# Attention ahead of two expert layers: chunks of both batches in turn, a packed state, and a new first order

## The chip, the cores and the metric

One core of one Trainium2 chip runs the whole program. The time is the device time of one execution in microseconds (us), and the number compared is the median of several executions.

## What is computed

The program chains three layers. First a retention-like attention: 2 batches, 8 heads, 768 tokens, head size 64. Then a gated expert layer behind an RMS normalization, then a layer with a leaky ReLU.

```
for t in range(S):
    state = gamma * state + outer(k[t], v[t])        # per batch and head, 64x64
    y[t] = scale * q[t] @ state
x = y as 1536 tokens x 512
xn = x / sqrt(mean(x*x) + 1e-6) * rms_g
x = (silu(xn @ w_gate) * (xn @ w_val)) @ w_out       # d_ff 1536
out = leaky(x @ w2_in) @ w2_out                      # d_ff 2048, leaky = max(0.01 h, h)
```

The activations are float32, the weights float64.

## The kernel before, in words

**Attention.** The 1536 tokens are cut into 12 chunks of 128, chunks 0 to 5 of batch 0 and 6 to 11 of batch 1. Each chunk c takes these steps: `scores` multiplies keys and queries into two PSUM banks (tile sc, L153); `decay_scores` on VectorE (DVE) multiplies them with the decay mask (a, L159); `decay_k`, `decay_q` and `decay_state` on GpSimd (POOL) make kd (L124), qs (L135) and tmp (L141); `outer` multiplies kd and v into u (L169); `update` on DVE makes the next state, u + tmp (L177, L179 for the first chunk of a batch); `heads` makes y from the old state (L186) and from a and v (L197); `squares` on ScalarE (ACT) writes y squared and y times rms_g (L211, L216). The eight heads are four pairs: state and u are 128x128 per pair, of which two 64x64 blocks on the diagonal count, so `update` takes two instructions of 64 partitions, and the rest of the state is zeroed once by memset (L848).

**Normalization.** For a pair of chunks `total` adds the squares over the features with products against ones (tot, L232), `mean` scales (na, L241), `rsqrt` makes 1/sqrt by a bit trick and three Newton steps, 13 instructions on POOL (nr and nt, L246 to L251). `spread` brings it back by products with the identity (bc, L257); `scaled` multiplies (xg, L274 on DVE) and rounds to the high part (xh, L275 on ACT); `rest` makes the low part (xl, L280 on DVE).

**Weights.** `fetch` loads one 128x512 tile of float64 (raw, L364) into one of three buffers; `start_unit` and `convert` turn it into a high and a low float32 part: two ACT instructions (L474, L475), four on DVE (L424, L428, L433, L442), the high part on ACT (L445), the low part on DVE (L449). Every float32 product is three: high by high, high by low, low by high.

**Expert layers.** The tokens form three blocks of 512. Block 0 of the first group of weights multiplies four pairs of gate and value tiles (g and v, 12 products of 128x512 each, L502), applies silu (L658), multiplies (L662), splits the result into go_h and go_l (L507, L508) and multiplies with the output weights (ao, L537). The weights of this group are converted while block 0 uses them. Blocks 1 and 2 follow. Later groups use a scheme with seven products in place of eight for blocks 1 and 2.

**Order.** All before block 0 is written out by hand under `manual_schedule` (from L871 on): chunks 0 to 5 up to their products, with 12 calls of `convert`. The rest of the attention is a list of tasks from `attention(6, (4, 5))`; the loop over `steps` hands out some of them after each step, so that the chunks of block 1 are done when its first product is due. There a scheduler sets the order of the instructions on each engine. Each engine runs its instructions in that order, and the DMAs are issued by SyncE (SP), in order too; a load waits there for its buffer. All loads of tables stand in SP's queue between the chunks.

Of the kernel before, what the change touches and what calls it, by code (L numbers as in the profile page):

```python
# [33 lines left out]
EARLY = 5  # L34
AHEAD = [4, 4]
PACE = 6
BLOCKS = [512, 512, 512]


@with_exitstack  # L40
def chain_kernel(ctx: ExitStack, tc: tile.TileContext, qk_t, kv, w1, w2, mask, qdec, kdec, sdec, rms_g, ident, out):
# [34 lines left out]
    state = [const.tile([P, NPAIR, P], F32, name=f"state{i}") for i in range(2)]  # L76
# [13 lines left out]

    ch = {}
    xh, xl, xg = {}, {}, {}
    n_loaded = [0]

    def load_chunks(upto):
        while n_loaded[0] < min(NCHUNK, upto):
# [4 lines left out]
            nc.sync.dma_start(out=a, in_=qk_t[c])  # L101
# [3 lines left out]
            nc.sync.dma_start(out=b, in_=kv[c])  # L105
# [11 lines left out]
    def last(c):  # L117
        return c % CPB == CPB - 1
# [12 lines left out]
    def decay_q(c):  # L131
        if c % CPB:
# [4 lines left out]
    def decay_state(c):  # L137
        if c % CPB and not last(c):
            s = ch[c]
            s["tmp"] = by_pair(scratch(f"tmp{c}"))  # L140
# [21 lines left out]
    def outer(c):  # L162
        if not last(c):
            s = ch[c]
            s["u"] = u = extra_bank(c, 2 + c % 2, f"u{c}")
            kd = s["kd"].rearrange("p h d -> p (h d)")
            for a in range(NPAIR):
                t = slice(a * P, (a + 1) * P)
                nc.tensor.matmul(out=u[:, t], lhsT=kd[:, t], rhs=s["kv"][:, 1, t], start=True, stop=True)  # L169

    def update(c, j):
        if not last(c):
            s = ch[c]
            r = slice(j * D, (j + 1) * D)
            new, u = state[c % 2][r, :, r], by_pair(s["u"])[r, :, r]
            if c % CPB:
                nc.vector.tensor_tensor(out=new, in0=u, in1=s["tmp"][r, :, r], op=ALU.add)  # L177
            else:
                nc.vector.tensor_copy(new, u)  # L179

    def heads(c):
        s = ch[c]
        s["y"] = y = extra_bank(c, c % 2, f"y{c}")
        inter = c % CPB != 0
        for a in range(NPAIR if inter else 0):
            nc.tensor.matmul(  # L186
                out=y[:, a * CH:(a + 1) * CH],
                lhsT=state[(c + 1) % 2][:, a, :],
                rhs=s["qs"][:, a, :],
                start=(a == 0),  # L190
                stop=False,
                skip_group_check=True,
            )
# [812 lines left out]
```

## Time and profile before

| | us |
|---|---|
| runs shown: 3, median | 618.07 |
| lowest to highest | 616.29 to 619.55 |
| the profiled execution | 619.15 |
| its span, first to last instruction | 617.3 |
| PE (TensorE products) busy | 601.5 (97%) |
| DVE busy | 444.5 (72%) |
| ACT busy | 322.5 (52%) |
| POOL busy | 68.0 (11%) |
| mean granted clock of TensorE | 0.994 |

The page names an engine's instructions by line and tile, gives their number, mean duration and the idle time before them with what ended it. Busy time of PE counts a product until its modelled end, so products in a row overlap. The granted clock is given as a share of full speed, 2.4 GHz; 0.5 is 1.2 GHz. The names after the arrow are what an instruction reads.

### The profile page before, as it was taken

How to read it: one execution, taken by the hardware profiler on the slowest of the kernel's cores; microseconds unless marked ns; L12 is line 12 of the kernel's file. 1: busy time of each engine (PE TensorE's matmuls, PEld its weight loads, DVE VectorE, ACT ScalarE, POOL GpSimd, SP SyncE). 2: the span in 40 equal slices, each digit the busy share in tenths (PEclk: the TensorE clock that was granted, in tenths of full speed). 3: DMA queues.
4: the chain of work that ended last, by engine and by line, in shares of the span. 5: the costliest groups of instructions: out<-in, count | busy, mean ns of one | idle time of the engine just before them, and what ended most of it. 6: DMA issues, size and time to landing. Idle time of an engine off the chain costs nothing.

```text
span 617.3 us, 7999 instructions
## 1 busy us (share of the span) xinstructions
PE 601.5 (97%) x2978; PEld 495.6 (80%) x2978; DVE 444.5 (72%) x766; ACT 322.5 (52%) x568; POOL 68.0 (11%) x128
## 2 busy tenths in 40 slices
PE   7979899999999999999999999999999999999997
PEld 5967677888888888888888888888888888888886
DVE  3697998466987859959778989975949694832243
ACT  2465663535675556455457556876755464423320
POOL 4853284310000000000000000000000000000000
PEclk9998999999999999999999999999999999999999
DMA  8845544100332122312312130323212120000013
GB/s 337 332 138 170 171 145 134 62 2 1 87 119 68 63 75 69 102 35 72 134 53 84 35 103 1 103 69 102 81 56 70 68 68 1 1 0 1 0 69 136
DMA packets 15877, 52.74 MB, mean 85 GB/s; under 512 B 2144, under 2 KB 2272, under 8 KB 15840
## 3 DMA queue, kind: packets, MB, share of 16 engines
q1 hardware_dynamic: 15840, 52.25, 25.0%
q8 instruction: 23, 0.38, 0.2%
q14 instruction: 14, 0.11, 0.1%
HBM read 49.09 MB, written 3.15 MB: 85 GB/s over the span
## 4 chain that ended last, share of the span: by engine, by line
PE 88%; DVE 5%; POOL 2%; DMA 2%; ACT 1%; issue 1%; SPq 0%; POOLq 0%; ACTq 0%; DVEq 0%
PE ap L537 21%; PE ao L537 15%; PE v L502 8%; PE g L502 8%; PE iX L698 7%; PE i L502 7%; PE iZ L698 4%; PE vX L698 4%; PE gX L698 4%; PE gZ L698 2%; PE vZ L698 2%; PE iY L698 2%; PE sc L153 1%; DMA raw_g<-in_w 1%; PE u L169 1%; PE y L197 1%
## 5 line engine op out<-in xcount | busy, mean ns | idle before, releaser
L502 PE MATMUL v<-xh,w_v 128*128 128x512 f32 x160 | 42.2, 405 | 0.9 <-ACT w_v L445 0.9
L502 PE MATMUL g<-xh,w_g 128*128 128x512 f32 x160 | 40.9, 394 | 2.0 <-ACT xg L216 1.1
L537 PE MATMUL ap<-w_p,gp_0h 128*128 128x512 f32 x128 | 39.4, 389 | 0.0
L537 PE MATMUL ap<-w_p,gp_1h 128*128 128x512 f32 x128 | 39.4, 389 | 0.0
L537 PE MATMUL ap<-w_p,gp_2h 128*128 128x512 f32 x128 | 39.4, 389 | 0.0
L502 PEld LDWEIGHTS g<-xh,w_g 128*128 128x128 f32 x160 | 29.7, 188 | 9.1 <-ACT xg L216 1.6
L502 PEld LDWEIGHTS v<-xh,w_v 128*128 128x128 f32 x160 | 30.5, 194 | 8.1 <-ACT w_v L445 1.1
L508 DVE TENSOR_TENSOR gp_0l<-i,gp_0h 128x512 fp32r<-128x512 f32 x16 | 11.0, 688 | 33.8 <-ACT gp_0h L507 33.8
L537 PE MATMUL ao<-go_0h,w_o 128*128 128x512 f32 x96 | 32.1, 395 | 0.0
L502 PE MATMUL i<-x2h,w_i 128*128 128x512 f32 x128 | 31.6, 389 | 0.0
L537 PE MATMUL ao<-go_2h,w_o 128*128 128x512 f32 x96 | 31.5, 389 | 0.0
L537 PE MATMUL ao<-go_1h,w_o 128*128 128x512 f32 x96 | 31.0, 390 | 0.0
L601 DVE TENSOR_TENSOR y2acc<-ap,y2acc 128x512 f32<-128x512 f32 x36 | 23.3, 686 | 10.4 <-PE ap L537 10.4
L537 PEld LDWEIGHTS ap<-w_p,gp_0h 128*128 128x128 f32 x128 | 24.0, 188 | 5.0
L537 PEld LDWEIGHTS ap<-w_p,gp_2h 128*128 128x128 f32 x128 | 24.0, 188 | 5.0
L537 PEld LDWEIGHTS ap<-w_p,gp_1h 128*128 128x128 f32 x128 | 24.0, 188 | 5.0
L502 PEld LDWEIGHTS i<-x2h,w_i 128*128 128x128 f32 x128 | 24.0, 188 | 5.0
L537 PE MATMUL ap<-w_p,gp_0l 128*128 128x512 f32 x64 | 24.9, 389 | 0.0
L537 PE MATMUL ap<-w_p,gp_1l 128*128 128x512 f32 x64 | 24.9, 389 | 0.0
L537 PE MATMUL ap<-w_p,gp_2l 128*128 128x512 f32 x64 | 24.9, 389 | 0.0
L662 DVE TENSOR_TENSOR g<-v,g 128x512 f32<-128x512 f32 x16 | 10.9, 684 | 17.8 <-PE v L502 17.8
L508 DVE TENSOR_TENSOR gp_2l<-hold,gp_2h 128x512 fp32r<-128x512 f32 x16 | 11.0, 688 | 15.8 <-ACT gp_2h L507 11.7
(240 smaller groups left out, 1588.3 us busy)
## 6 DMA issues: line engine op xcount, KB each, us to landing
raw_i<-in_w SPq DMA_DIRECT2D x16, 512.0 KB, 3.5
raw_p<-in_w SPq DMA_DIRECT2D x16, 512.0 KB, 3.6
qkT<-in_qk_t SPq DMA_DIRECT2D x12, 512.0 KB, 4.8
kv<-in_kv SPq DMA_DIRECT2D x12, 512.0 KB, 5.7
raw_g<-in_w SPq DMA_DIRECT2D x12, 512.0 KB, 3.5
raw_v<-in_w SPq DMA_DIRECT2D x12, 512.0 KB, 3.5
raw_o<-in_w SPq DMA_DIRECT2D x12, 512.0 KB, 3.4
out<-y2acc SPq DMA_DIRECT2D x12, 256.0 KB, 2.2
```

What stands on the lines that cost most here:

```text
L153: nc.tensor.matmul(out=s["sc"][j][:, t], lhsT=k_[r, t], rhs=q_[r, t], start=True, stop=True)
L169: nc.tensor.matmul(out=u[:, t], lhsT=kd[:, t], rhs=s["kv"][:, 1, t], start=True, stop=True)
L197: nc.tensor.matmul(out=y[j * D:(j + 1) * D, a * CH:(a + 1) * CH], lhsT=s["kv"][:, 1, e:e + D], rhs=s["a"][j][:, a, :], start=not inter, st ...
L502: nc.tensor.matmul(out=dst, lhsT=lhs, rhs=rhs, start=(n == 0), stop=(n == len(pairs) - 1))
L508: nc.vector.tensor_tensor(out=l[:, :T], in0=x, in1=h[:, :T].bitcast(F32), op=ALU.subtract)
L537: nc.tensor.matmul(out=acc["b"][m], lhsT=lhs, rhs=rhs, start=(start and n == 0), stop=(stop and n == 2))
L601: nc.vector.tensor_tensor(out=dst, in0=banks[m], in1=dst, op=ALU.add)
L662: nc.vector.tensor_tensor(out=a, in0=x, in1=a, op=ALU.mult)
L698: nc.tensor.matmul(out=dst, lhsT=lhs, rhs=rhs, start=(start and n == 0), stop=(n == 5), skip_group_check=True)
```

## The change

- **Chunks in turn.** Position c of the sequence is now chunk `c % 2 * 6 + c // 2`: even positions are batch 0, odd ones batch 1. The state of position c comes from c-2; there are four state tiles. The output rows follow.
- **Packed state.** State, tmp and u hold 64 columns per pair. `outer` makes eight 64x64 products per chunk in place of four of 128x128; the part of `heads` from the state makes eight of 64x64 tiles in place of four; `update` is one instruction of 128x256; tmp is 128x256. The memsets of the state are gone.
- **1/sqrt.** For block 0 it runs on VectorE, a seed and three Newton steps of three instructions, per pair of chunks. For blocks 1 and 2 it stays on POOL, now once per four chunks.
- **First order.** Five small tables are loaded from ACT's queue. Chunks 0 to 4 stand ahead of block 0, with 16 calls of `convert`; chunk 5 comes with block 0. The tasks of one chunk follow the letters of TASKS.
- **Products of zeros.** `heat` multiplies a tile of zeros, 128x128 by 128x512 in bfloat16. Besides the ten at the start, 23 stand between the instructions ahead of block 0.

```diff
-EARLY = 5
+EARLY = 4
+TASKS = "Lthoknqdus"
+LATE = 4
...
+    def chunk_of(c):
+        return c % 2 * CPB + c // 2
...
-                out=s["tmp"], in0=state[(c + 1) % 2], in1=sdec_sb.to_broadcast([P, NPAIR, P]), op=ALU.mult
+                out=s["tmp"], in0=state[(c - 2) % 4], in1=sdec_sb.to_broadcast([P, NPAIR, D]), op=ALU.mult
...
-                nc.tensor.matmul(out=u[:, t], lhsT=kd[:, t], rhs=s["kv"][:, 1, t], start=True, stop=True)
+                for j in range(2):
+                    e = slice(a * P + j * D, a * P + (j + 1) * D)
+                    nc.tensor.matmul(
+                        out=u[j * D:(j + 1) * D, a * D:(a + 1) * D],
+                        lhsT=kd[:, e],
+                        rhs=s["kv"][:, 1, e],
+                        start=True,
+                        stop=True,
+                    )
...
+            u = s["u"][:, :NPAIR * D].rearrange("p (a e) -> p a e", a=NPAIR)
+            new = state[c % 4]
...
+    def newton(cs, g=nc.vector):
+        a, r, t = (nrm[cs][m] for m in ("a", "r", "t"))
+        if g is nc.vector:
+            g.scalar_tensor_tensor(out=t, in0=r, scalar=-0.5, in1=r, op0=ALU.mult, op1=ALU.mult)
+            g.tensor_tensor(out=t, in0=t, in1=a, op=ALU.mult)
+            g.scalar_tensor_tensor(out=r, in0=t, scalar=1.5, in1=r, op0=ALU.add, op1=ALU.mult)
+            return
...
-            if c < NCHUNK and c % 2:
-                due = (c - 1, c)
+            if c < NCHUNK and c % 4 == 3:
+                due = (c - 3, c - 2, c - 1, c)
...
+            def heat():
+                nc.tensor.matmul(out=wb, lhsT=warm[:, :P], rhs=warm, start=True, stop=True)
...
+            outer(2), convert(1), decay_k(3), heat(), scores(3), decay_state(2), update(2), heat(), decay_q(3)
+            convert(1), convert(1), convert(1), heads(2), dsc(3), outer(3), decay_state(3), decay_k(4)
...
+            heat(), seed(PAIR1), newton(PAIR1), heat(), newton(PAIR1), newton(PAIR1), convert(1)
+            scaled(PAIR0, 0), heat(), scaled(PAIR0, 1), convert(1), heat(), spread(PAIR1), heat()
...
-        tasks, complete = attention(6, (4, 5))
+        tasks, complete = attention(5, None)
```

On DVE, from the last scaling of block 0 to the first value weight, the order before is this (a6 is the masked scores of chunk 6, wa and wb the work tiles of a weight, w_v0 the first value weight):

```order
L274 TENSOR_TENSOR xg0_185<-xg0_185,bc2_469 128x4x128 x2
L280 TENSOR_TENSOR xl0_433<-xg0_185,xh0_432 128x4x128 x4
L428 TENSOR_SCALAR wa_v0_270<-wa_v0_270 128x512
L449 TENSOR_TENSOR w_g0_233<-wa_g0_234,w_g0_233 128x512
L433 SCALAR_TENSOR_TENSOR wa_v0_270<-raw_v0_132,wa_v0_270 128x512
L159 TENSOR_TENSOR a6_0_557<-sc6_0_547,mask_sb_94 128x512
L159 TENSOR_TENSOR a6_1_559<-sc6_1_548,mask_sb_94 128x512
L442 ISA wa_v0_270<-wa_v0_270,wb_v0_271 128x1024
L424 TENSOR_SCALAR wa_o0_504<-wa_o0_504 128x512
L424 TENSOR_SCALAR wa_g1_571<-wa_g1_571 128x512
L428 TENSOR_SCALAR wa_o0_504<-wa_o0_504 128x512
L449 TENSOR_TENSOR w_v0_351<-wa_v0_270,w_v0_351 128x512
```

The same stretch on DVE in the changed kernel (L304 is the scaling, L310 the low part, L476 the step that adds the low bits to a weight, L483 the low part of a weight, bc2 the spread 1/sqrt of positions 2 and 3):

```order
L304 TENSOR_TENSOR xg0_238<-xg0_238,bc0_443 128x4x128 x2
L467 SCALAR_TENSOR_TENSOR wa_v0_299<-raw_v0_143,wa_v0_299 128x512
L304 TENSOR_TENSOR xg0_238<-xg0_238,bc2_492 128x4x128
L196 TENSOR_TENSOR state0_101<-u4_398,tmp4_421 128x256
L304 TENSOR_TENSOR xg0_238<-xg0_238,bc2_492 128x4x128
L310 TENSOR_TENSOR xl0_482<-xg0_238,xh0_481 128x4x128
L458 TENSOR_SCALAR wa_g1_565<-wa_g1_565 128x512
L310 TENSOR_TENSOR xl0_482<-xg0_238,xh0_481 128x4x128 x2
L476 ISA wa_v0_299<-wa_v0_299,wb_v0_300 128x1024
L310 TENSOR_TENSOR xl0_482<-xg0_238,xh0_481 128x4x128
L458 TENSOR_SCALAR wa_o0_433<-wa_o0_433 128x512
L483 TENSOR_TENSOR w_v0_410<-wa_v0_299,w_v0_410 128x512
```

The low part of the gate weight (L483 for w_g0) stands directly ahead of these rows, where before it stood behind the low parts of x; the masked scores of position 5, which stood ahead, and those of position 6 now follow behind.

On PE, inside block 0, the 1/sqrt of block 1 before comes in two pairs; the second pair is spread here (ao is the output product, bc6 the spread 1/sqrt of chunks 6 and 7, g3 the fourth gate product):

```order
L197 MATMUL y8_946<-a8_1_821,kv8_624 64x128
L537 MATMUL ao_0_0_3_792<-go_1_0h_763,w_o1_667 128x512
L257 MATMUL bc6_999<-ident_sb_99,nr6_885 128x128 x2
L502 MATMUL g3_0_1019<-xh0_432,w_g3_850 128x512 x8
L502 MATMUL g3_0_1019<-xl0_433,w_g3_850 128x512 x4
```

In the changed kernel one spread of four stands on PE (bc4 is the 1/sqrt of positions 4 to 7, v2 the third value product):

```order
L571 MATMUL ao_0_0_0_842<-go_1_0h_829,w_o1_666 128x512
L571 MATMUL ao_0_0_0_842<-go_1_0l_830,w_o1_666 128x512
L571 MATMUL ao_0_0_0_842<-go_1_0h_829,w_o1_666 128x512
L571 MATMUL ao_0_0_1_843<-go_1_0h_829,w_o1_666 128x512
L287 MATMUL bc4_979<-ident_sb_99,nr4_923 128x128 x4
L536 MATMUL v2_0_995<-xh0_481,w_v2_764 128x512 x8
L536 MATMUL v2_0_995<-xl0_482,w_v2_764 128x512 x4
```

The four sums it depends on stand on PE behind the third gate product g2; between those sums and these rows stand all products of position 8 and the scores of position 9. Behind the spread stands the third value product, and then all of g3; before, v2 stood ahead of the spread.

## Rows read from the trace of the kernel before

**Rows 1.** Windows: start:end, length; busy us and instructions per engine; clock, DMA share, GB/s.

```profile
36.00:46.00 10.00, 7.21 (x51) 5.74 (x48) 10.00 (x15) 7.67 (x18) 5.44 (x6) 0.97 0.61 191
46.00:53.00 7.00, 7.00 (x27) 5.26 (x25) 3.48 (x7) 3.20 (x6) 3.66 (x13) 0.55 0.51 151
53.00:98.00 45.00, 40.86 (x277) 33.03 (x276) 42.96 (x70) 25.34 (x50) 21.80 (x28) 1.00 0.50 164
...
106.00:140.00 34.00, 33.96 (x172) 28.26 (x171) 19.89 (x30) 15.83 (x30) 10.76 (x31) 1.00 0.13 45
140.00:600.00 460.00, 460.00 (x2029) 380.39 (x2028) 333.55 (x587) 251.96 (x426) 0.00 (x0) 1.00 0.18 60
```

**Rows 2.** Timeline of PE: start us, us, instruction, idle before and releaser.

```profile
39.62 1.86 PE L502 MATMUL g<-xh,w_g 128*128 128x512 f32 x7 [0.80 <-DVE w_g L449]
...
47.01 3.35 PE L502 MATMUL v<-xh,w_v 128*128 128x512 f32 x7
...
87.02 0.71 PE L257 MATMUL bc<-ident_sb,nr 128*128 128x128 f32 x4 [1.28 <-POOL nr L251]
...
106.06 2.12 PE L502 MATMUL g<-xh,w_g 128*128 128x512 f32 x8
```

**Rows 3.** Timeline of DVE, same columns.

```profile
44.62 0.68 DVE L449 TENSOR_TENSOR w_v<-wa_v,w_v 128x512 fp32r<-128x512 f32 x1
45.22 0.68 DVE L433 SCALAR_TENSOR_TENSOR wa_o<-raw_o,wa_o 128x512 int32<-128x512 int32 x1
45.82 0.41 DVE L428 TENSOR_SCALAR wa_g<-wa_g 128x512 int32<-128x512 int32 x1
46.16 0.68 DVE L442 CUSTOM_DVE_ANT_0 wa_o<-wa_o,wb_o 128x1024 uint16<-128x1024 uint16 x1
...
52.10 0.69 DVE L662 TENSOR_TENSOR g<-v,g 128x512 f32<-128x512 f32 x1 [3.29 <-PE v L502]
...
98.15 0.68 DVE L662 TENSOR_TENSOR g<-v,g 128x512 f32<-128x512 f32 x1
```

**Rows 4.** Groups of DVE, 36 to 98 us: busy us, mean ns, then idle before.

```profile
L159 DVE TENSOR_TENSOR a<-sc,mask_sb 128x512 f32<-128x512 f32 x10 | 6.5, 679 | 0.3 <-PE sc L153 0.3
L449 DVE TENSOR_TENSOR w_o<-wa_o,w_o 128x512 fp32r<-128x512 f32 x4 | 5.0, 1254 | 1.4 <-ACT w_o L445 1.4
...
L177 DVE TENSOR_TENSOR state<-u,tmp 64x256 f32<-64x256 f32 x5 | 2.1, 413 | 0.0
```

**Rows 5.** Group of DVE over the whole span.

```profile
L449 DVE TENSOR_TENSOR w_i<-wa_i,w_i 128x512 fp32r<-128x512 f32 x16 | 11.0, 688 | 9.1 <-ACT w_i L445 9.1
```

**Rows 6.** Groups of PE over the whole span: products of the attention.

```profile
L197 PE MATMUL y<-a,kv 128*64 128x128 f32 x192 | 13.1, 279 | 0.2 <-DVE a L159 0.2
...
L169 PE MATMUL u<-kv,kd 128*128 128x128 f32 x80 | 11.6, 284 | 2.3 <-POOL kd L124 2.3
```

**Rows 7.** Groups of POOL over the whole span.

```profile
L135 POOL TENSOR_TENSOR qs<-qkT,qdec_sb 128x512 f32<-128x512 f32 x10 | 13.2, 1318 | 9.1 <-PE y L186 5.3 <-DMA qkT<-in_qk_t 2.5 <-POOL kd L124 1.3
...
L124 POOL TENSOR_TENSOR kd<-kv,kdec_sb 128x512 f32<-128x512 f32 x10 | 10.6, 1060 | 17.9 <-PE u L169 8.5 <-DMA kdec_sb<-in_kdec 5.7 <-DMA kv<-in_kv 3.7
...
L251 POOL TENSOR_TENSOR nr<-nr,nt 128x2 f32<-128x2 f32 x18 | 6.8, 377 | 1.5
```

**Rows 8.** Group of DVE, 0 to 36 us: the smallest operand.

```profile
L241 DVE TENSOR_SCALAR na<-tot 128x2 f32<-128x2 f32 x2 | 0.3, 160 | 4.5 <-PE tot L232 4.5
```

**Rows 9.** Timeline of POOL: ends of the longest 1/sqrt chain.

```profile
79.70 0.51 POOL L246 TENSOR_SCALAR nr<-na 128x2 int32<-128x2 int32 x1
...
84.10 2.86 POOL L251 TENSOR_TENSOR nr<-nr,nt 128x2 f32<-128x2 f32 x1
```

**Rows 10.** Timeline of PE: four per-token sums of two chunks.

```profile
20.27 1.95 PE L232 MATMUL tot<-ones,sq 128*128 128x1 f32 x16
```

**Rows 11.** Chain that ended last: start us, us, what; a load, twelve products of a group.

```profile
2.11 5.13 DMA kdec_sb<-in_kdec
...
145.36 2.72 PE v L502 x12
```

More of the change, by code (lines that the diff above doesn't have):

```diff
@@ L75, in chain_kernel @@
     ones = const.tile([P, 1], F32, name="ones")
-    state = [const.tile([P, NPAIR, P], F32, name=f"state{i}") for i in range(2)]
+    state = [const.tile([P, NPAIR, D], F32, name=f"state{i}") for i in range(4)]
     def bank(name):
@@ L131, in decay_q @@
     def decay_q(c):
-        if c % CPB:
+        if not opens(c):
             s = ch[c]
@@ L137, in decay_state @@
     def decay_state(c):
-        if c % CPB and not last(c):
+        if not opens(c) and not last(c):
             s = ch[c]
-            s["tmp"] = by_pair(scratch(f"tmp{c}"))
+            s["tmp"] = at.tile([P, NPAIR, D], F32, tag="tmp", name=f"tmp{c}")
             nc.gpsimd.tensor_tensor(
-                out=s["tmp"], in0=state[(c + 1) % 2], in1=sdec_sb.to_broadcast([P, NPAIR, P]), op=ALU.mult
+                out=s["tmp"], in0=state[(c - 2) % 4], in1=sdec_sb.to_broadcast([P, NPAIR, D]), op=ALU.mult
             )
@@ L183, in heads @@
         s["y"] = y = extra_bank(c, c % 2, f"y{c}")
-        inter = c % CPB != 0
+        inter = not opens(c)
         for a in range(NPAIR if inter else 0):
[L186 to L193, printed above, removed]
+            for j in range(2):
+                r = slice(j * D, (j + 1) * D)
+                nc.tensor.matmul(
+                    out=y[r, a * CH:(a + 1) * CH],
+                    lhsT=state[(c - 2) % 4][r, a, :],
+                    rhs=s["qs"][r, a, :],
+                    start=(a == 0),
+                    stop=False,
+                    skip_group_check=True,
+                )
         for a in range(NPAIR):
@@ L846, in chain_kernel, with load_qdec, load_ident @@
         nc.vector.memset(ones, 1.0)
-        for s in state:
-            nc.gpsimd.memset(s, 0.0)
-        for c in range(5):
-            load_chunks(c + 1)
-            if c == 0:
-                nc.sync.dma_start(out=kdec_sb, in_=kdec)
-                nc.sync.dma_start(out=sdec_sb, in_=sdec)
-                nc.sync.dma_start(out=g_sb, in_=rms_g)
-            elif c == 1:
-                nc.sync.dma_start(out=qdec_sb, in_=qdec)
-            else:
-                fetch()
-            if c == 2:
-                nc.sync.dma_start(out=ident_sb, in_=ident)
-        def upd(c):
-            update(c, 0)
-            update(c, 1)
+        nc.scalar.dma_start(out=kdec_sb, in_=kdec)
+        nc.scalar.dma_start(out=g_sb, in_=rms_g)
+        nc.scalar.dma_start(out=sdec_sb, in_=sdec)
+        load_chunks(1)
+        def load_qdec():
+            nc.scalar.dma_start(out=qdec_sb, in_=qdec)
+        def load_ident():
+            nc.scalar.dma_start(out=ident_sb, in_=ident)
         def dsc(c):
@@ L870, in chain_kernel @@
         with tc.manual_schedule():
-            wb = bank("warm_up")
+            wb = acc_bank(3, "warm_up")
+            def heat():
+                nc.tensor.matmul(out=wb, lhsT=warm[:, :P], rhs=warm, start=True, stop=True)
             for _ in range(WARM):
-                nc.tensor.matmul(out=wb, lhsT=warm[:, :P], rhs=warm, start=True, stop=True)
+                heat()
             PAIR0, PAIR1 = (0, 1), (2, 3)
-            scores(0), dsc(0), decay_k(0), outer(0), heads(0), squares(0), upd(0)
```

83 lines of the change are left out of this document (44 added, 39 removed).

## The prediction

> **What bounds the kernel now.** I read the windows first [rows 1]. From 140 to 600 us TensorE (PE) is busy all the time, from 106 to 140 but for 0.04 us, so nothing that happens there to another engine shows in the end, and the change leaves these products as they are. What can move is the moment at which block 1 begins on PE, 106.06 us [rows 2]; the rest follows at a fixed distance. Ahead of it stands block 0, and there VectorE (DVE) is the bound: 42.96 of the 45 us from 53 to 98 and all of 36 to 46, while PE has 40.86 of 45 and 7.21 of 10.
>
> The DVE timeline gives the landmarks [rows 3]: the low part of the first value weight w_v ends at 45.30, the first of the four products silu(g) times v stands at 52.10, the fourth at 98.15. The rows between 44.62 and 46.16 also give the pace of DVE when nothing disturbs it: 0.60 us from one 128x512 instruction of two tensors to the next, 0.34 for one with a scalar.
>
> From 52.10 to 98.15 DVE works off 47 of the first kind (8 steps L442, 8 L433, 9 L449, 8 masked scores, 14 of scaling, splitting and multiplying), 16 of the second and 7 half states of 0.42 [rows 4]: 28.2 + 5.4 + 2.9 = 36.5 us. It took 46.05. Some 2 us are waits; about 7 are stretched instructions. The groups show which: L449 takes 0.688 us in the later stages, where POOL rests [rows 5], and 1.254 in block 0 for w_o, while the masked scores, with one input in PSUM, stay at 0.679 [rows 4]. So in block 0 DVE pays 0.19 us on each us of work while POOL is busy 21.80 of 45 us [rows 1].
>
> There is a second loss. In the window from 46 to 53 the granted clock is 0.55 [rows 1], so near 1.2 GHz for most of it, after a stretch in which PE had waited 2.8 of 10 us. The value product at 47.01 takes 3.35 us for 7 [rows 2], where a full group of 12 later takes 2.72 [rows 11]. DVE waits 3.29 us for it at 52.10 [rows 3]. The price is 0.45 x 7 = 3.2 us of PE.
>
> **The change, part by part.** Durations are of the profiled execution (619.15 us, 0.2% over the median of 618.07); I work out a shift and put it on the median.
>
> *Up to block 0.* PE works nearly without a pause from its warm-up (5.1 us) on. A chunk's own products take 13.1 / 12 = 1.1 us, the scores, of equal number, I take the same [rows 6]. Scores and own products of five chunks: 11. Products from the state for positions 2 to 5: 4 x 1.1. Outer products: 6 u, before 11.6 / 10 = 1.16 each [rows 6]; now 16 records with half the columns, between 0.6 (half) and 1.1 (16 records like y); I take 0.85: 5.1. Sums: 16 records took 1.95 us [rows 10], so 3.9 for four chunks; two spreads of 0.7 [rows 2]; 23 products of zeros at 2.72 / 12 = 0.23 [rows 11]: 5.2. Sum 31; waits for the first kd and for the second chunk's masked scores (DVE now copies that chunk's state first), about 2 us: the first gate product at about 38. Before it ran at 39.62 [rows 2], because w_g was late. The zeros cost nothing while DVE is later still; without that cover they would cost up to 5.
>
> The 1/sqrt takes 10 instructions per pair on DVE in place of 13 on POOL; a DVE instruction on 128x2 takes 0.16 [rows 8] and POOL's last step of a Newton round 0.377 in the mean [rows 7]: 1.6 in place of 4.9 us at the same rate for all. On DVE there is room: two na alone found it idle for 4.5 us [rows 8].
>
> *The first value weight.* Behind bc2, on PE four zeros, one state product and one u ahead of 38, so at 35.2, DVE has eight long instructions (two scalings, four low parts, L476, L483), two short ones, a state and, from L476 to L483, a wait for the high part on ACT, taken as one long instruction: 4.8 + 0.7 + 0.4 + 0.6 = 6.5: 41.7, against 45.30. Two short, seven long and one state follow up to the first product: 47.0, with some stretching 47.5, against 52.10. PE reaches the end of the first value product at 44.5, so it is no longer the later one, and has little reason for the slow clock.
>
> *Block 0.* The last thing that PE waits for on DVE is the second half of the masked scores of position 9. Up to it stand 45 long, 16 short and 2 states: 27.0 + 5.4 + 0.8 = 33.2. POOL does less in all (a tmp of half the width, 26 small instructions gone), but in this stretch it has three qs of 1.32, three kd of 1.06, one 1/sqrt of 13 x 0.377 [rows 7], together 12, and eight shorter instructions of up to 0.5: 16 of 33 us, the same share as before. So I keep the 0.19: 39.5. To it comes the wait for the spread of four, estimated at 1.5: 13 steps at 0.377 and one qs between them make 6.2, less the 5 us of products that stand ahead of bc4 on PE. End: 88.5.
>
> *To block 1.* Behind it PE has the own products of position 9 (1.1), u (0.85), scores (1.1), v3 (2.72), all products of position 10 (2.2), ao (2.72), scores (1.1) and the state product of position 11 (1.1): 12.9 in all, so 101.4. Before, block 1 began at 106.06 with that last part still to come, so 4.7 + 1.1 = 5.8 us are gained.
>
> *The tables.* The first link of the chain that ended last is the load of kdec, issued at 2.11 and landed 5.13 later [rows 11]; the first u waits 2.3 for kd [rows 6]. From ACT's queue kdec is issued over 1 us earlier, and nothing stands ahead of it there. By these rows alone the start could come up to 2.3 sooner, a sum of 610. I count nothing: kd needs kv of the first chunk too, which stands third in SP's queue as before. The Trainium skill (DMA: Bandwidth & Descriptors, Issuing engines are not separate DMA queues) speaks against a gain as well: loads issued by SP and ACT run on the same 16 engines and interleave, so a second queue brings no bandwidth. By that rule the sum stays.
>
> *Nothing for the rest.* ACT has no work ahead of the first y; five issues hide there. The memsets lay where POOL waits for kdec [rows 7]. The halves of the states saved (0.42 per chunk) are in the counts. In block 1 DVE is busy 19.89 of 34 us [rows 1], so the 1/sqrt for block 2 in one go has room; without it, block 2 would begin with a stall like the one at bc4.
>
> Sum: 618.07 - 5.8 = 612.3, taken as **612.3 us** (613.4 for an execution like the profiled one). The bounds: stretching of 0 to 0.25 (-6 to +2 us), the wait at bc4 0 to 5 (-1.5 to +3.5), u (-1 to +1), the tables (-2 to 0), the early clock loss (0 to +3).
>
> **Rivals.**
> *A. PE becomes the bound (605).* If the stretching goes with POOL's smaller work, DVE is ahead of PE, and PE's own sum rules: from 38 on, 132 products of 0.227 = 29.9 and the attention of positions 5 to 11, 26: block 1 at 94, a gain of 13. For it: PE is already busy 40.86 of 45. Against: POOL's share in the stretch is unchanged.
> *B. The small steps on DVE collide (616.5).* The new Newton steps read two tiles of SBUF, and such instructions stretched [rows 4]. In their stretch POOL has two kd, one qs and one tmp, some 4.2 us [rows 7]; if each holds DVE up once in full, the first weights come 4.2 later: a gain of 1.6. Against: POOL waits for the old qs to be read there. [...]
> *C. The spread of four stalls PE (621, slower).* bc4 stands in PE's queue ahead of v2 and g3, so nothing hides a late 1/sqrt. The longest chain before ran from 79.70 to 86.96 [rows 9]; with its slow first steps throughout, the long step of 2.86 and one qs it would be 11.8 us, a wait of 7.1, 5.6 more than counted. A wait like that can bring the low clock, 3.2 [rows 1]: 8.8 - 5.8 = 3.0 slower. It decides from a chain of 9 us on, and only if the clock falls too.
> *D. The zeros don't keep the clock (615.5).* They end where block 0 begins, and before it fell ten us into block 0. The same 3.2 us then stay: a gain of 2.6.
>
> **How the numbers follow.** A measurement of this kernel can tell about 0.5%, 3.1 us, from no change. Forecast 0.48, A 0.14, B 0.15, C 0.08, D 0.15. Faster by more: under 615.0, most of the forecast (0.44), A, and a third of D and of B with their errors, 0.68. Slower: most of C, 0.07. The rest, 0.25, within. The range takes A's end and B's: 605 to 617.5; it leaves out C and the far ends, about 0.15.
>
> **What would show it.** Right: the first product on DVE near 47.5, the fourth value product's end near 94, block 1 near 101, PE full from there, clock 1.00 from 40 to 53. L449 for w_o still above 1 us; under 0.8 and block 1 at 94 would be A. Wrong: nr's last step on DVE after 34 (B), PE idle over 4 us ahead of bc4 (C), a window under 0.9 behind 38 (D), or PE idle behind block 1, which no case has.

## The result and the profile after

The change makes the kernel slower: 625.52 us median against 618.86 for the kernel before in the same session, ratio 1.0104 (95% interval 1.0072 to 1.0136); 612.3 was forecast. The profiled execution took 624.75, its span is 622.8, its mean granted clock 0.989.

The windows of after, with the columns of [rows 1]: busy us and instructions of PE, PEld, DVE, ACT and POOL, then TensorE's granted clock, DMA share and GB/s.

```profile
24.00:28.00 4.00, 4.00 (x41) 3.37 (x43) 3.83 (x11) 0.99 (x2) 2.17 (x3) 0.67 0.46 145
...
36.00:46.00 10.00, 8.15 (x71) 5.71 (x70) 9.89 (x15) 4.81 (x10) 4.64 (x5) 1.00 0.30 101
46.00:53.00 7.00, 5.87 (x52) 4.37 (x51) 7.00 (x13) 5.40 (x11) 0.99 (x1) 1.00 0.91 299
53.00:98.00 45.00, 36.67 (x302) 29.96 (x302) 38.90 (x65) 24.46 (x52) 24.18 (x29) 0.89 0.52 176
106.00:140.00 34.00, 34.00 (x195) 27.82 (x192) 18.32 (x24) 14.66 (x29) 6.95 (x18) 1.00 0.08 28
...
76.00:80.00 4.00, 4.00 (x50) 3.80 (x48) 4.00 (x11) 3.50 (x7) 2.37 (x1) 0.57 0.96 339
...
84.00:88.00 4.00, 1.07 (x5) 1.07 (x6) 0.00 (x0) 0.00 (x0) 3.42 (x11) 0.50 0.52 198
88.00:92.00 4.00, 4.00 (x17) 3.36 (x17) 2.95 (x5) 2.23 (x5) 1.01 (x2) 0.73 0.16 65
```

The low clock of 46 to 53 us in [rows 1] is gone. In its place PE and DVE both lose over 4 us between 53 and 98, and from 84 to 88 DVE does nothing, PE nearly nothing, while POOL works and the clock stands at 0.50. The clock is low in two more places where it was 1.00 before: from 24 to 28 (0.67) and from 76 to 80 (0.57, behind a wait of 1.28 us at 75.06). From 106 on PE is full again, as before: block 1 begins at 111.79 and the span ends 511.0 us later (before 511.2, [rows 2]). So the loss lies ahead of block 1.

The timeline of PE of after, at the places of [rows 2]: start, duration, instruction, and the idle time ahead of it with what ended it.

```profile
38.73 2.11 PE L536 MATMUL g<-xh,w_g 128*128 128x512 f32 x8
...
43.34 1.20 PE L536 MATMUL g<-xl,w_g 128*128 128x512 f32 x4 [1.85 <-DVE xl L310]
...
86.93 2.08 PE L287 MATMUL bc<-ident_sb,nr 128*128 128x128 f32 x8 [5.50 <-POOL nr L276]
88.66 2.80 PE L536 MATMUL v<-xh,w_v 128*128 128x512 f32 x8
...
101.38 2.11 PE L536 MATMUL v<-xh,w_v 128*128 128x512 f32 x8 [0.87 <-DVE state L196]
...
111.79 0.50 PE L536 MATMUL g<-xh,w_g 128*128 128x512 f32 x1
```

The spread of four, bc4, waits 5.50 us for nr, the 1/sqrt, on POOL. Then it takes 2.08 us in place of the 1.05 that eight such records take at clock 1.00 (e9, below), and v2 runs slowly behind it (2.80 for eight in place of 2.11). The timeline of POOL shows the 1/sqrt:

```profile
77.64 3.98 POOL L264 TENSOR_SCALAR nr<-na 128x4 int32<-128x4 int32 x1 [4.71 <-DVE na L260]
81.70 0.20 POOL L273 TENSOR_TENSOR nt<-nr 128x4 f32<-128x4 f32 x1
...
83.05 1.71 POOL L145 TENSOR_TENSOR qs<-qkT,qdec_sb 128x512 f32<-128x512 f32 x1
...
86.68 0.20 POOL L276 TENSOR_TENSOR nr<-nr,nt 128x4 f32<-128x4 f32 x1
```

And the timeline of DVE, first ahead of and at the places of [rows 3], then beside that 1/sqrt:

```profile
38.53 1.51 DVE L458 TENSOR_SCALAR wa_g<-wa_g 128x512 f32<-128x512 f32 x1
39.96 2.13 DVE L310 TENSOR_TENSOR xl<-xg,xh 128x512 fp32r<-128x512 f32 x2
...
43.55 0.68 DVE L483 TENSOR_TENSOR w_v<-wa_v,w_v 128x512 fp32r<-128x512 f32 x1
...
50.58 0.68 DVE L696 TENSOR_TENSOR g<-v,g 128x512 f32<-128x512 f32 x1
...
77.40 0.14 DVE L260 TENSOR_SCALAR na<-tot 128x4 f32<-128x4 f32 x1
77.47 0.67 DVE L483 TENSOR_TENSOR w_o<-wa_o,w_o 128x512 fp32r<-128x512 f32 x1
78.07 0.67 DVE L476 CUSTOM_DVE_ANT_0 wa_g<-wa_g,wb_g 128x1024 uint16<-128x1024 uint16 x1
...
81.15 0.41 DVE L462 TENSOR_SCALAR wa_o<-wa_o 128x512 int32<-128x512 int32 x1
81.49 0.67 DVE L169 TENSOR_TENSOR a<-sc,mask_sb 128x512 f32<-128x512 f32 x1
...
89.05 2.48 DVE L304 TENSOR_TENSOR xg<-xg,bc 128x512 f32<-128x512 f32 x4 [5.41 <-PE bc L287]
...
95.43 0.68 DVE L169 TENSOR_TENSOR a<-sc,mask_sb 128x512 f32<-128x512 f32 x1
```

POOL's seed, the first step of the 1/sqrt on a tile of four columns, becomes ready behind na at 77.40, starts in the trace at 77.64 and ends at 81.62. DVE runs eight instructions in a row from 77.47, all with operands in SBUF; the first that reads PSUM starts at 81.49, and 0.13 us later the seed is done.

### The profile page after: what moved, and what is told of

Same layout as the page of the kernel before. It is cut to its first block, busy times and chain, and to the rows that moved or that the text cites. A ratio compares the mean times of both kernels' runs of the same rounds, so it can differ in the third digit from the quotient of the medians.

```text
span 622.8 us, 8304 instructions
## 1 busy us (share of the span) xinstructions
PE 602.7 (97%) x3160; PEld 492.6 (79%) x3160; DVE 444.6 (71%) x774; ACT 322.3 (52%) x568; POOL 54.9 (9%) x74
## 4 chain that ended last, share of the span: by engine, by line
PE 87%; DVE 6%; DMA 2%; POOL 1%; issue 1%; ACT 0%; ACTq 0%; SPq 0%; POOLq 0%; DVEq 0%
PE ap L571 21%; PE ao L571 15%; PE g L536 8%; PE v L536 8%; PE iX L732 7%; PE i L536 7%; PE iZ L732 3%; PE vX L732 3%; PE gX L732 3%; PE gZ L732 2%; PE iY L732 2%; PE vZ L732 2%; DMA kv<-in_kv 2%; PE y L216 1%; DMA qdec_sb<-in_qdec 1%
## 5 line engine op out<-in xcount | busy, mean ns | idle before, releaser
L536 PE MATMUL v<-xh,w_v 128*128 128x512 f32 x160 | 40.7, 397 | 2.4 <-DVE a L169 1.6
L542 DVE TENSOR_TENSOR gp_0l<-i,gp_0h 128x512 fp32r<-128x512 f32 x16 | 11.0, 687 | 33.8 <-ACT gp_0h L541 33.8
L635 DVE TENSOR_TENSOR y2acc<-ap,y2acc 128x512 f32<-128x512 f32 x36 | 23.3, 685 | 10.4 <-PE ap L571 10.4
L536 PE MATMUL g<-xl,w_g 128*128 128x512 f32 x80 | 21.5, 391 | 1.9 <-DVE xl L310 1.9
```

What stands on the lines that cost most here:

```text
L536: nc.tensor.matmul(out=dst, lhsT=lhs, rhs=rhs, start=(n == 0), stop=(n == len(pairs) - 1))
L542: nc.vector.tensor_tensor(out=l[:, :T], in0=x, in1=h[:, :T].bitcast(F32), op=ALU.subtract)
L635: nc.vector.tensor_tensor(out=dst, in0=banks[m], in1=dst, op=ALU.add)
```

## The experiments

Theory T1: the 1/sqrt of four chunks on POOL stalls PE and brings the low clock. Rival R: the new first order costs. Rival V: DVE's queue bounds block 0 whatever the 1/sqrt does. Block 1 is the start of its first gate product in the profiled execution; before 106.06, after 111.79. In every profile the span ends 511 to 513 us behind it. It is the reading of one execution each, and so is the clock: of ten profiles with the whole first order of after, eight have the clock at 1.00 from 20 to 36 us and the first gate product at 37.1 to 37.7, while after and e6 have 0.89 and 38.7. Up to 1.6 us of a difference in block 1 can therefore come from ahead of block 0; the ratios, from medians, are the measure.

| run | change to | ratio to before, 95% | block 1 |
|---|---|---|---|
| e1 | after | 1.0037 (1.0011 to 1.0063) | 108.75 |
| e2 | after | 1.0182 (1.0144 to 1.0220) | 117.00 |
| e3 | after | 1.0089 (1.0055 to 1.0122) | 110.94 |
| e4 | after | 1.0095 (1.0065 to 1.0126) | 109.86 |
| e5 | after | 1.0021 (0.9990 to 1.0052) | 107.25 |
| e6 | after | 1.0034 (1.0009 to 1.0059) | 108.47 |
| e7 | after | 1.0029 (1.0002 to 1.0056) | 108.19 |
| e8 | before | 0.9928 (0.9890 to 0.9967) | 100.69 |
| e9 | e8 | 0.9978 (0.9946 to 1.0010) | 104.24 |
| e10 | e5 | 1.0134 (1.0084 to 1.0185) | 112.73 |
| e12 | e8 | 0.9939 (0.9908 to 0.9969) | 101.05 |
| e13 | e8 | 0.9999 (0.9971 to 1.0026) | 103.95 |
| e14 | e5 | 1.0083 (1.0053 to 1.0113) | 107.70 |
| e15 | e9 | 0.9964 (0.9928 to 1.0000) | 101.73 |
| e16 | e8 | 0.9890 (0.9858 to 0.9922) | 103.03 |
| e17 | e5 | 0.9996 (0.9977 to 1.0014) | 104.12 |
| e18 | e5 | 1.0030 (1.0010 to 1.0050) | 106.50 |
| e19 | e14 | 0.9976 (0.9959 to 0.9992) | 102.69 |

### The 1/sqrt of four: e1, e3, e5, e6, e7

**e1**, in `rsqrt`, POOL to DVE:

```diff
-        seed(cs, nc.gpsimd)
+        seed(cs)
         for _ in range(NEWTON):
-            newton(cs, nc.gpsimd)
+            newton(cs)
```

> The changed kernel, but the 1/sqrt of the four chunks of block 1 (and of block 2) is also done on VectorE, 10 instructions in place of 13 on GpSimd. Nothing else moves. Theory T1 (the seed of 1/sqrt waits 3.98 us on GpSimd behind VectorE's work, the chain of 9.5 us lets TensorE stand 5.5 us ahead of the spread bc4, and the low clock follows): the wait ahead of bc4 falls under 1.5 us, no window between 70 and 98 us has a clock under 0.85, block 1 begins at 104 to 107 in place of 111.8, and the time is 617 to 621, ratio to the kernel before 0.997 to 1.004. Rival R (the new first order is what costs: the late first weights and the clock that fell at 25 us): the wait goes, but VectorE, the bound of block 0, is no earlier; block 1 begins at 110 to 112, ratio 1.008 to 1.012. Rival V (VectorE is the bound and the 10 instructions only add to it): ratio 1.010 to 1.014.

It gains 0.67%, at the edge of what T1 said; R and V both said nothing would come. But block 1 is later than T1 had it (and 1.5 of its 3.0 us over after stand already at the first product on DVE, 49.08 against 50.58), the clock from 76 to 98 us is 0.81, and a wait is left, now for DVE:

```profile
84.84 2.04 PE L287 MATMUL bc<-ident_sb,nr 128*128 128x128 f32 x8 [3.50 <-DVE nr L271]
```

The scheduler puts a conversion behind each of the ten steps, so the chain from na (75.89) to nr (84.69) is 8.8 us long here too.

**e3** opens a gap for POOL:

```diff
+        if n == 4:
+            for _ in range(4):
+                nc.vector.tensor_scalar(w["t"], w["tot"][:, :n], 1.0 / DM, EPS, ALU.mult, ALU.add)
```

> The changed kernel with four short VectorE instructions added behind the mean of chunks 4 to 7; they read the sums from PSUM and write a small tile that is overwritten later, so they cost VectorE some 0.65 us and nothing else moves. Theory T1 in its narrow form (GpSimd's seed doesn't get at SBUF while VectorE runs instruction after instruction with two SBUF inputs; an instruction that reads PSUM lets it in): the seed ends within 1 us in place of 3.98, the 1/sqrt 3 us sooner, the wait ahead of bc4 falls from 5.5 to about 2.5, ratio 1.001 to 1.007. Rival (GpSimd's seed was slow by itself, or waits for something else): seed 3 to 4 us as before, ratio 1.010 to 1.013.

The narrow theory holds, its price does not. In the timelines of DVE and POOL of e3 an added step reads PSUM at 76.90 and the seed ends at 77.02, after 0.63 us; but kd then comes between the steps of POOL:

```profile
76.90 0.15 DVE L263 TENSOR_SCALAR nt<-tot 128x4 f32<-128x4 f32 x1
...
76.39 0.63 POOL L267 TENSOR_SCALAR nr<-na 128x4 int32<-128x4 int32 x1 [4.71 <-DVE nt L263]
...
79.80 1.49 POOL L134 TENSOR_TENSOR kd<-kv,kdec_sb 128x512 f32<-128x512 f32 x1
...
86.25 0.20 POOL L279 TENSOR_TENSOR nr<-nr,nt 128x4 f32<-128x4 f32 x1
```

In this build's order kd, sq and ss stand in POOL's queue between the Newton steps, with qs 4.8 us of other work (in after qs alone, 1.71), and bc4 still waits 4.74. The added instructions cost too: POOL waited 0.50 us for their tile, PE 0.85 for their bank. So the run shows what held the seed, not what its release is worth.

**e5** gives the sums, the mean and the DVE steps priority (`with tc.high_priority():` around them).

> The changed kernel with the 1/sqrt of blocks 1 and 2 on VectorE, and the sums, mean and 1/sqrt of a block given priority in the scheduler, so that the mean stands between the two masked scores of position 8, five long instructions sooner than in e1. In e1 the chain from the mean to the last step took 8.8 us because a conversion stood behind each of its steps; it does so here too, but begins some 1.5 to 2 us sooner. Theory T1 (what is left of the loss is the wait ahead of bc4, 3.5 us in e1, and the clock that falls with it): the wait is 0 to 1.5 us, block 1 begins at 104 to 107, ratio to before 0.993 to 1.001. Rival V (block 0 is bound by VectorE's work, whatever bc4 waits for): block 1 at 108 to 110 as in e1, ratio 1.002 to 1.006.

The 1/sqrt ends at 81.89, and bc4 still waits 4.33 us, for ACT's copies of y that free its bank at 82.7. **e6** sets `TASKS = "Lthokqdusn"`, so bc4 stands behind v2; **e7** is e5 and e6 together.

> The changed kernel, 1/sqrt on GpSimd as there, but the spread of four and what follows it stand last in each round of attention tasks: on TensorE bc4 comes behind the value product v2 (2.72 us) instead of ahead of it. Theory T1: the wait ahead of bc4 falls by about 2.7 us, to 2.5 to 3.5, and the value product no longer waits for it, ratio 1.003 to 1.008. Rival V (VectorE bounds block 0): VectorE only gets its scaling work later, ratio 1.008 to 1.012.

> e5 and e6 together: 1/sqrt on VectorE with priority, and the spread of four behind the value product. Theory T1: no wait of over 1 us ahead of bc4, no window between 76 and 98 us with a clock under 0.95, block 1 at 102 to 105, ratio 0.990 to 0.997, which is the forecast made for the change itself (0.991). Rival V: block 1 at 108 to 110, ratio 1.002 to 1.006.

In e6, with the 1/sqrt left on POOL, bc4 waits half as long and the gain is that of e1; its clock from 24 to 28 is that of after (0.68), so its 3.3 us at block 1 owe nothing to the start:

```profile
86.24 1.49 PE L287 MATMUL bc<-ident_sb,nr 128*128 128x128 f32 x8 [2.73 <-POOL nr L276]
```

e7 gains no more than either: bc4 waits for nothing, but v2 now waits 4.05 us, released by a state update that stands on DVE behind the Newton steps and conversions:

```profile
82.32 3.78 PE L543 MATMUL v<-xh,w_v 128*128 128x512 f32 x8 [4.05 <-DVE state L196]
```

So undoing what T1 names gives back 0.7 to 0.8%, and e7 fits V's account of the rest: where bc4's wait goes, another of some 4 us comes up that DVE's queue releases late. How much of it is the wait and how much the low clock, no run separates.

### Parts that cost nothing, or more when undone: e2, e4, e10

**e2** has `due = (c - 1, c)` for odd c, pairs again; **e10** does the same to e5.

> The changed kernel, but sums, 1/sqrt and spread of chunks 4 and on are done for two chunks at a time, as before, with the 1/sqrt still on GpSimd. Theory T1: the first pair's 1/sqrt starts some 10 us sooner and has less behind it, and only two spreads hang on it; but the seed of GpSimd can still be held by VectorE, as 2.86 us were in the kernel before. The wait ahead of the first spread is 0 to 3 us, block 1 begins at 105 to 109, ratio 0.998 to 1.006. Rival R (the first order costs, not the four in one): block 1 at 110 to 112, ratio 1.008 to 1.012.

> The changed kernel with pairs in place of fours and the 1/sqrt on VectorE with priority: e5 and e2 together. In e2 the first pair's 1/sqrt on GpSimd let TensorE wait 7.0 us. Theory T1 (GpSimd's 1/sqrt is what made e2 slow, and pairs are better than fours): no wait of over 2 us ahead of a spread, block 1 at 101 to 105, ratio 0.990 to 0.999. Rival R (the new first order and VectorE's order behind it cost, so no way of doing the 1/sqrt brings it back): ratio 1.001 to 1.008.

Both are slower than fours, against T1's expectation. In e10 the spreads wait 2.68 and 1.95 us and the value or gate products behind both run slowly (3.56 and 3.22 us for eight); in e2 the first spread waits longer than any other in these runs:

```profile
65.23 1.22 PE L287 MATMUL bc<-ident_sb,nr 128*128 128x128 f32 x4 [7.00 <-POOL nr L276]
```

The likely reason is that in the new order of steps each spread stands on PE where it waits, so two of them stall twice; no run tests that by itself. **e4** drops the `heat()` of the first order. There are 22 of them, not the 23 named ahead of the result and below: the trace of after has 32 products of zeros, with the ten at the start.

> The changed kernel without the 23 products of zeros in the first order; the ten of the warm-up stay. If they only fill waits and keep the clock: the first gate product no earlier than 37, clock of the stretch from 20 to 50 us lower by 0.1 or more, ratio to the kernel before 1.010 to 1.020. If they delay TensorE: the first gate product up to 5 us sooner (34 to 36), block 1 sooner by 1 to 4 us, ratio 1.003 to 1.009. If neither (VectorE bounds block 0 and the products of zeros change nothing): ratio 1.009 to 1.012.

1.0095 against 1.0104: no difference, though block 1 came 1.9 us sooner in this one profile. The first gate product came 0.9 us sooner than in after (37.80), but later than in the eight profiles with zeros and clock 1.00 from 20 to 36 us; e4 and after both have 0.89 there. The zeros make no difference to the time that the runs can tell. Whether they keep the clock there is not shown: one profile without them has the fall, and so have two of ten with them.

### One part alone on the kernel before: e8, e9, e15, e12, e13

**e8** takes only the packed state, its outer products, products from the state, update and tmp:

```diff
-                t = slice(a * P, (a + 1) * P)
-                nc.tensor.matmul(out=u[:, t], lhsT=kd[:, t], rhs=s["kv"][:, 1, t], start=True, stop=True)
+                for j in range(2):
+                    e = slice(a * P + j * D, a * P + (j + 1) * D)
+                    nc.tensor.matmul(
+                        out=u[j * D:(j + 1) * D, a * D:(a + 1) * D],
+                        lhsT=kd[:, e],
+                        rhs=s["kv"][:, 1, e],
...
```

> The kernel before with one part of the change alone: the state in 64x64 tiles of two heads over all 128 partitions, so 16 narrow outer products a chunk in place of 4 wide ones, one state update on VectorE of 0.42 us in place of two, half the tmp on GpSimd, no memsets of the state. The first order, the pairs and the chunks' sequence stay. If VectorE bounds block 0, as the prediction has it: 7 half states of 0.42 and GpSimd's lighter load give 3 to 4 us, block 1 at 102 to 104, ratio 0.993 to 0.997. If the extra products cost TensorE more than the copies save: ratio 1.000 to 1.004. If it is hidden: 0.998 to 1.001.

This gains 0.72%, a shade more than the first of the three said, and block 1 comes 5.4 us sooner, not the 2 to 4 it said:

```profile
100.69 1.65 PE L511 MATMUL g<-xh,w_g 128*128 128x512 f32 x6
```

The groups of PE and DVE (36 to 98 us) of e8 against [rows 4, 6]:

```profile
L170 PE MATMUL u<-kv,kd 128*64 128x64 f32 x160 | 7.1, 227 | 2.2 <-POOL kd L124 2.2
...
L184 DVE TENSOR_TENSOR state<-u,tmp 128x256 f32<-128x256 f32 x4 | 1.7, 413 | 0.0
L458 DVE TENSOR_TENSOR w_o<-wa_o,w_o 128x512 fp32r<-128x512 f32 x4 | 3.3, 822 | 1.4 <-ACT w_o L454 1.4
```

The outer products take 7.1 us in place of 11.6, one state update does what two did, and w_o is stretched to 0.82 us in place of 1.25.

**e9** adds the fours to e8 (`due = (c - 3, c - 2, c - 1, c)`, first due None); **e15** adds DVE and priority to that, as in e5.

> e8 (the kernel before with the packed state alone) with one more part of the change: sums, 1/sqrt on GpSimd and spread of block 1's four chunks in one, behind the fourth, in place of two pairs. The first order and the sequence of chunks are those of the kernel before. Theory T1 (four in one is a loss wherever it stands): TensorE waits 3 to 6 us ahead of bc4, the 1/sqrt takes over 6 us on GpSimd, block 1 begins 3 to 6 us later than the 100.7 of e8, ratio to before 0.998 to 1.004. Rival R (the loss is tied to the new first order, the pairs cost nothing and gain nothing): block 1 within 1.5 us of e8, ratio 0.991 to 0.995.

> e9 (packed state, the old first order, block 1's four chunks normalised in one) with the 1/sqrt on VectorE and priority, as in e5. In e9 TensorE did not wait ahead of bc4, but later for weights (0.69 and 1.97 us), after VectorE had done four scalings in a row, and the clock fell. If four in one costs by that bunching on VectorE and not by GpSimd's chain: ratio 0.996 to 1.001, as e9 or worse. If by GpSimd's chain: 0.991 to 0.995, as e8.

Block 1 comes 3.6 us later in e9 than in e8, without any wait at bc4. PE waits for weights: 0.69 us ahead of DVE's four scalings, behind stretched conversions, and 1.97 us behind them. The timeline of PE of e9:

```profile
79.14 1.05 PE L266 MATMUL bc<-ident_sb,nr 128*128 128x128 f32 x8
...
90.28 3.35 PE L511 MATMUL v<-xh,w_v 128*128 128x512 f32 x7 [1.97 <-DVE w_v L458]
```

e15 can't be told from e9, so with the old order of steps POOL's chain does no harm that the runs can tell: na stood there at 71.95, 7.2 us ahead of its spread, with other products between. What the fours cost there, some 0.4 to 0.5%, is put down to bunching on DVE; the intervals of e8, e9 and e15 don't settle that it is a cost, and no run tests the bunching.

**e12** puts the 1/sqrt of block 0 on DVE in e8 (`rsqrt(PAIR0, nc.vector)`, the same for PAIR1); **e13** puts 5 and 10 products of zeros into PE's waits from 37 to 46 us.

> e8 with the 1/sqrt of block 0's two pairs on VectorE, 10 instructions each, in the first order of the kernel before: a second part of the change alone. If the step of the prediction holds (some 2 us on VectorE in place of 4.6 to 7 on GpSimd, with VectorE idle there): the second spread 2 to 4 us sooner, the first gate product 35 to 37 in place of 38.8, block 1 at 98 to 99.5, ratio 0.986 to 0.990. If the small steps collide with GpSimd or the first weights are late anyhow: ratio 0.991 to 0.996.

No gain, the second case: the wait for the first gate weight grew from 1.12 to 2.35 us, and the gate products came no sooner (38.81 in e8):

```profile
39.94 1.42 PE L522 MATMUL g<-xh,w_g 128*128 128x512 f32 x5 [2.35 <-DVE w_g L469]
```

> e8 with 15 products of zeros in TensorE's waits from 37 to 46 us: 5 ahead of the first gate product and 10 ahead of the first value product (one accumulator bank for the outer products in place of two makes room for them). If a clock that falls behind a wait costs what the prediction says (3.2 us at 46 to 53): the window 46 to 53 has a clock over 0.9 in place of 0.63, the value product takes 2.7 in place of 4.9 us, the first product on VectorE comes at 48.5 to 49.5 in place of 51.6, ratio 0.987 to 0.990. Rival (VectorE bounds what follows, so a faster TensorE there waits later): block 1 within 1 us of e8, ratio 0.991 to 0.995. If the clock falls all the same: as e8, or up to 2 us later.

The windows of e13 from 36 to 106 show a clock kept where it was wanted and lost again later:

```profile
46.00:53.00 7.00, 6.67 (x41) 5.20 (x40) 7.00 (x15) 4.21 (x7) 3.51 (x7) 1.00 0.84 257
53.00:98.00 45.00, 40.78 (x335) 31.61 (x333) 40.88 (x69) 26.60 (x55) 23.16 (x37) 0.96 0.47 161
98.00:106.00 8.00, 7.11 (x59) 6.10 (x60) 4.29 (x8) 1.54 (x3) 5.09 (x15) 0.79 0.53 189
```

The first product on DVE came 2.3 us sooner than in e8 (49.24), yet block 1 came 3.3 us later: a spread waited 2.00 us and a sum 2.76, both for POOL. The edit also took one of two PSUM banks from the outer products, so what of this is due to the zeros stays open.

### The order of the steps: e14, e17, e18, e19

**e14** is e5 with position 5 back in the first order (`scores(5), dsc(5), outer(5), heads(5)` and the rest of it in place of 9 of the 22 `heat()`, then `attention(6, None)`).

> e5 (the changed kernel with the 1/sqrt of blocks 1 and 2 on VectorE, with priority) and the products of position 5 back in the first order, as the kernel before has it, where they take the place of 11 of the 23 products of zeros. Theory M (the new first order moved position 5, some 4 us of TensorE and 1.7 us of VectorE, into block 0 and did not end sooner for it, because VectorE's low parts and the first weight bound its end; zeros fill the gap): the first gate product within 1.5 us of the 37.1 of e5, block 1 3 to 5 us sooner than the 107.3 of e5, ratio 0.993 to 0.998. Rival (VectorE and TensorE lose in the first order what they save in block 0): first gate product at 39.5 to 42, ratio 1.000 to 1.004.

Slower still than the rival said: seven of the eight gate products begin at 40.01, where all eight began at 37.14 in e5, and block 1 is no earlier. What block 0 saves, the first order loses, so theory M falls.

```profile
40.01 1.91 PE L543 MATMUL g<-xh,w_g 128*128 128x512 f32 x7
...
107.70 1.65 PE L543 MATMUL g<-xh,w_g 128*128 128x512 f32 x6
```
**e18** lowers the pace of conversions on e5 (`PACE = 4` in place of 6). **e17** gives the steps of a position the order of the kernel before, on e5, outer products and sums first and the spread last; **e19** does the same on e14:

```diff
-TASKS = "Lthoknqdus"
+TASKS = "otLkqdhsun"
```

> e5 (the changed kernel, 1/sqrt of blocks 1 and 2 on VectorE with priority) with the attention steps of a position handed out in the order of the kernel before: outer products and sums first, then load, scores, masked scores, own products, squares, state, and the spread last. On VectorE some six conversion steps of later weights then stand behind the masked scores of positions 8 and 9 and not ahead of them. If the new order of these steps is what is left of the loss: the third product on VectorE at 83 to 85 in place of 88.5, block 1 at 102 to 105, ratio 0.993 to 0.999. If the first order or the sequence of chunks is: ratio 1.000 to 1.005, as e5.

> e14 (e5 with position 5 back in the first order) with the attention steps in the order of the kernel before, as in e17. What is left of the change against e15 (0.996) is then the first order itself, the chunks in turn from both batches and the loads. If the order of the steps is the cause: ratio 0.993 to 0.999, as e15. If the first order or the sequence is: 1.003 to 1.010, as e14.

> e5 with the pace of conversions 4 in place of 6: per step of block 0 fewer conversion steps are handed out ahead of need. If VectorE's conversions of later weights ahead of block 0's own work are what is left of the loss: ratio 0.995 to 1.000. If the weights only come later where they are needed (w_v and w_o of the fourth pair): ratio 1.002 to 1.010.

With position 5 in the first order the order of the steps is worth 1.1% (e19 against e14, intervals apart); without it 0.25%, which the intervals don't settle. In e19 block 1 comes 5.0 us sooner than in e14, bc4 waits for nothing, and no window from 76 on is under 1.00. e18 brings nothing: 1.0030, and bc4 waits 4.42 us as in e5.

**e16**, with the lowest median, hands out three more conversion steps in the first order of e8, ahead of its low parts (`convert(3), rest(0), rest(1), rest(2), rest(3)`).

> e8 with three conversion steps of the first order moved ahead of the four low parts xl, so that the low part of the first gate weight comes 2.5 us sooner on VectorE. In e8 TensorE waits 1.1 us for it, then 1.5 and 1.1 for what follows. If the first weights bound the end of the first order: the seven gate products at 37 to 38 in place of 38.8, block 1 at 99 to 100, ratio 0.988 to 0.992. If the order of block 0 on VectorE, which the scheduler builds anew, decides: anything from 0.991 to 1.000.

It takes 611.5 us median, 1.1% less than before and 2.1% less than after (0.9890 / 1.0104 = 0.979). Its profiled execution took 616.25 at clock 0.986, with 0.50 from 24 to 28, so its 103.03 doesn't stand for the median, and that it beats e8 is not shown: the intervals overlap.

## Why the prediction was wrong

**What bounds, and where: right.** Everything is decided ahead of block 1, and DVE's work up to the second half of the masked scores of position 9 was forecast at 39.5 us and measured 95.43 + 0.68 - 50.58 - 5.41 (its wait for bc4) = 40.1. The sum held better than its parts: the low part of w_o took 0.76 us in the mean where "still above 1" was the sign, and the stretching sat on other instructions (L467 for wa_v 0.95, the low part of go_0 0.96).

**Block 0, the wait for the spread of four: the step that failed most.** It was put at 1.5 us, from 13 steps of 0.377 and one qs, 6.2 together, less 5 of products. The chain took 9.5 (77.40 to 86.88), of which the seed 3.98, and DVE stood 5.41: 3.9 more. The products covered only 4.0 of the chain, since na, which ends the mean, came 3.6 us after the sums had ended on PE (72.84 + 0.95), in DVE's queue. The row that showed the hold was there: the 2.86 us of nr in [rows 9] ended when DVE first read PSUM again, and the text took it for one slow step. In the timeline of DVE before, five instructions with operands in SBUF fill that time:

```profile
84.09 0.67 DVE L449 TENSOR_TENSOR w_g<-wa_g,w_g 128x512 fp32r<-128x512 f32 x1
...
86.93 0.43 DVE L177 TENSOR_TENSOR state<-u,tmp 64x256 f32<-64x256 f32 x1
```

By the Trainium skill (SBUF — State Buffer, Who interferes with whom) an instruction of DVE with two SBUF inputs and one of POOL that reads SBUF exclude each other. The traces agree, and show more: the seed was held over eight DVE instructions in a row, three of them with one SBUF input (L462 twice, L458). The prediction priced what POOL does to DVE, at 0.19 us on each us of work, and not what DVE does to POOL.

**The first value weight: 3.1 us too early.** Forecast 41.7 and 47.5, measured 44.23 and 50.58. Of the 3.1, 1.1 lie ahead: the scaling behind bc2 began at 36.34 in place of 35.2, in an execution whose clock fell from 24 to 28. In the eight profiles with the same first order and the clock at 1.00 there, the first product came at 47.3 to 49.9. The rest is stretching. The instructions were counted rightly, 11.2 us of undisturbed work from 36.34 to the first product; they took 14.2, so 3.0 in place of the 0.5 put in, while the 0.6 for a wait on ACT fell away. The largest parts are L458, with one SBUF input, 1.51 in place of 0.41 us, and two xl, 2.13 in place of 1.28. The same section of the Trainium skill says that one SBUF input doesn't contend outside DVE's two-port modes, and that `tensor_scalar` can enter these. No row here names the mode; the durations fit the exception.

**To block 1: 2.8 too short.** 12.9 forecast, 15.7 measured (96.1 to 111.79). PE had become the later one behind its stall: g3 ran until 96.84, the state products of position 9 still stood behind it, v3 waited 0.87, and some own products of position 11 began ahead of the gate product. With the start 3.1 later, the wait 3.9, this 2.8 and 0.6 of DVE's work the sum is 10.4, the distance from the forecast 101.4 to 111.79. Behind block 1 the forecast had 1.1 us less to come than before; the span ends 511.0 behind it in place of 511.2, so 0.9 more is missing. Together 11.3: from the 613.4 forecast for an execution like the profiled one to 624.75.

**1/sqrt on DVE: worth nothing.** It ended at 33.8, as said, but e12, with the old first order, shows that the first gate weight is then waited for instead.

**The zeros cost nothing: right (e4). The tables, 0: right.** That there are 22 zeros takes 0.2 us from the sum. The first kd waited for kdec until 7.38 before and waits for kv until 7.26 now: as the text said, kd needs kv too. The Trainium skill's rule there (DMA: Bandwidth & Descriptors, Issuing engines are not separate DMA queues) is neither borne out nor refuted by that. The packed products were put at 0.85 us a chunk and take 0.71. e8 shows that this part alone brings 4.5 us. That this is near the whole 5.8 forecast is chance: the forecast had 4.6 of them ahead of the first product on DVE, where e8 gains 0.5 (51.56 against 52.10); its gain comes between that product and block 1, where the forecast had none.

**The rivals.** C is what happened, with its mechanism, its place and its point (a chain over 9 us, PE idle 5.50, and the clock fell, to 0.50): 8% was too little. Its 621 was 4.5 short, since it kept the gain of 5.8 ahead of the stall. B's collisions are there, on two steps of a Newton round (0.56 and 0.54 in place of 0.16) and more on the conversions and low parts, the stretching above. D is not borne out in after, whose clock is 1.00 from 36 to 53 and falls elsewhere. But in six of the eight profiles just named (e1, e2, e3, e5, e7, e10) it falls where D has it, to 0.64 to 0.75 from 44 to 48, and DVE's first product waits 0.84 at most for that, not 3.29 as before: the price was wrong. e13 points the same way, as far as its second change allows: what the clock gave back at 46 was lost again behind later waits. A never came near.

What the runs show in place of the sum, step by step from before: packed state 0.993 (e8), fours 0.996 to 0.998 (e15, e9), new first order with chunks in turn 0.998 (e19), position 5 into block 0 1.000 (e17), new order of steps 1.002 (e5), 1/sqrt on POOL without priority 1.010 (after). Only the first and the last of these steps are clear of their intervals; how much the fours, the first order, the move of position 5 and the order of the steps each cost is not settled.

## What to carry to other kernels

A short chain of small steps on an engine that a busy neighbour can hold up may take as long as the neighbour's run of instructions, not as long as its steps; look for its longest row in the trace and for what the neighbour did until its end. Several results that are gathered into one chain save instructions on an engine with time to spare and put all who wait for them behind one moment. When a change has many parts, time each alone: here one part held the gain and the others together ate it. And read a place in one profile against other profiles with the same code there: here a fall of the clock moved the start by up to 1.6 us.

## What was not expected of the hardware

A POOL instruction on 128x4 elements took 3.98 us beside eight DVE instructions in a row and 0.63 beside a row with short PSUM reads in it (e3); a kd in e9, 1.04 us elsewhere, took 4.04 (58.11 to 62.15), beside DVE instructions without a gap until 61.24. With the stall of 5.5 us on PE the granted clock was 0.50, the lower level of 1.2 GHz, and it was 0.73 still in the four microseconds behind it, from 88 to 92; it had been 0.57 from 76 to 80, behind a wait of 1.28. Eight outer products onto 64x64 tiles take PE 0.71 us a chunk where four onto 128x128 took 1.16, less than the 0.85 taken.
